# Block-sparse attention with a routed MLP on one core: where direct pairs are summed, and how selection flags are turned

## The chip, the cores and the metric

One core of a Trainium2 chip runs one launch of the kernel. The metric is the device time of that launch in microseconds (us), less is better. Before the change it is 269.96 us, the median of three runs (269.89 to 271.47).

## The reference, cut to what matters

Attention over 4 batches of 8 heads, 768 positions, head dimension 64. Keys are grouped into 24 chunks of 32. From the minimum and maximum of each chunk an upper bound of each query's scores is made; each query keeps its 6 best chunks. Its output, as 3072 rows of 512, goes through a mixture of 8 experts with at most 80 rows each. In outline:

```
ub = np.sum(np.maximum(q[..., None, :] * k_min[:, :, None], q[..., None, :] * k_max[:, :, None]), axis=-1)
ub = np.where(causal, ub, -1e9)
top_chunks = np.argsort(ub, axis=-1)[..., -6:]
scores = np.where(sel & causal_position, scale * q @ k.T, -1e9)
attn = np.exp(scores - max) ; attn = attn / (attn.sum(-1) + 1e-9)
x = (attn @ v) as rows of 512
e = argmax(x @ w_gate); keep the 80 rows of highest gate weight per expert
out[rows] = gate * (relu(x @ w1[e]) @ w2[e])     # other rows are 0
```

## The kernel before, in words

**Pairs.** Two heads make a pair, four pairs a batch, sixteen pairs (0 to 15) the attention. The loop `for i in range(NP)` (L1218) is written out at build time; the order of its calls is the order of each engine's queue. `Sync.op` (L72) records what each instruction reads and writes and puts in the waits; engines otherwise run their queues in order. All of pair i+1's preparation runs beside pair i.

**One pair.** A pair's scores are made transposed, keys on partitions and queries on columns, in six stages (`STEPS`, L179). For each stage `scores` (L575) issues TensorE matmuls of keys by queries (`score_mm`, L572, or L560 in half tiles), adds MASKV to the chunks that a query has not selected by a second matmul (`flags`, L594: the table of blocks `ind` by the turned flags `unsT`), and lets ScalarE write the exponential to EXB (L604). Score buffers SC0 and SC1 alternate, so stage 2 can write SC0 only when the exponential of stage 0 has read it. For early pairs a 512-column score matmul of stages 0 and 1 is issued as two of 256 (L566). GpSimd then masks the diagonal block (`select`, L656 and L653) and adds the stages up into ES, one 768-column sum per head (`fold`, L672; the pieces are listed in `ADDS`, L190); some adds are VectorE's (`own_fold`, L675). `values` (L707) multiplies the exponentials by v on TensorE (L717) in twelve groups, and ScalarE copies the two parts of the output to oT (`values_out`, L725). `sums` (L744) makes, in the next pair's turn, the rows' denominators from ES (L753) and the routing logits from oT (L730) in the accumulator M0; its last matmul frees ES, into whose first tile GpSimd's first mask of the next pair writes.

**Short and direct pairs.** Pairs 1 to 5, 8, 9 and 13 are short: their last two stages share buffers in a tighter order, and `rows` (L801), which turns the previous pair's output, comes between the first score matmuls and their flags. Pairs 5, 9 and 13 are direct: `fold` leaves two of their adds out, which `sums` makes up for by matmuls that read the exponentials themselves (L748). After a direct pair, stage 2 of the next pair is issued before `sums` (L1226, L1227), its mask and fold later (L1245).

**Flags.** For the next pair, TensorE computes the bounds (`bounds`, L483); in `bounds_out` VectorE transposes them, finds the six best by MAX8 (L497) and writes the flags of unselected chunks to `uns` (L502): for each of five query tiles and each head a block of 64 columns of which 24 count. `unselT` (L505) turns them: for pairs 1 to 15 ten TensorE transposes (five tiles by two heads, L521) into MB, and one ScalarE copy of 640 columns to `unsT` (L523). `unselT(i + 1)` is called after `values(i)` (L1322), so the copy queues on ScalarE behind the values' second output copy. The next user is `flags` of stage 0 of pair i+1. Pair 0 has a turn of its own (L512, L517), with two copies of 384 and 256 columns.

**Routing.** Between the stages stand pieces of the previous batch's routing: VectorE's compares (`rank_cmp`, L931, and `rank_diag`, L924) at the end of the second pair of a batch, the counting matmuls that read them (`rank_count`, L1062) in the third pair, `rank_late` (L1076 and after) on VectorE, and table matmuls (L1085) in the fourth. In the last batch's third pair (14) the table comes after the values.

**Start.** POOL writes the block table `ind` from 64 partitions at a time (L419, L421) while the first loads run; ScalarE's first work of pair 0 is L454. After pair 15, a tail gathers the selected rows and runs the eight experts (`up`, L1457; `down`, L1483).

## Time and profile before

| what | value |
|---|---|
| median of the runs (3) | 269.96 us |
| the profiled execution, own time | 270.17 us |
| its span in the trace | 268.2 us |
| TensorE's granted clock, all 40 slices | 9 tenths or more of full speed (2.4 GHz) |
| busy share: TensorE / VectorE / GpSimd / ScalarE | 95% / 80% / 77% / 58% |
| DMA engines' mean busy share | near 90% until the tail |

The profile is of one execution. Times in a timeline are us from the span's start; PE is TensorE's matmul side, PEld its weight loads (which run ahead of the matmuls), DVE VectorE, ACT ScalarE, POOL GpSimd, SP the load queue. A row of a timeline may merge several instructions of one line (xN): its first number is when the first starts, its second from there to the end of the last. A float32 matmul is two instructions. What stands in brackets is how long the engine was idle before and what released it; with several waits the one that came last.

### The profile page before, as it was taken

To read this page: it belongs to the slowest core of one execution; us is meant where nothing else is said; L and a number is where in the kernel's file an instruction comes from. 1 tells how busy PE (TensorE), PEld (TensorE's weight loads), DVE (VectorE), ACT (ScalarE), POOL (GpSimd) and SP (SyncE) were. 2 spreads that over 40 slices of the span, in tenths; PEclk is the share of its full clock that TensorE was granted. 3 is DMA by queue.
4 is the path that set the end of the run, shared out by engine and by line. 5 is a ranking of instruction groups with operands and counts; after the bars stand their busy time and mean duration, and the time that the engine had idled before them with its cause. 6 is when DMAs were issued, how large, how long until landed. Compare 5 with 4: busy or idle time off the path is not lost.

```text
span 268.2 us, 9821 instructions
## 1 busy us (share of the span) xinstructions
PE 256.0 (95%) x4152; PEld 167.2 (62%) x4152; DVE 214.8 (80%) x587; ACT 155.4 (58%) x243; POOL 207.6 (77%) x291
## 2 busy tenths in 40 slices
PE   7799999999999999999999999999999999988993
PEld 7367676767676565666665666666556557664663
DVE  6878787687989988859899889999998998953242
ACT  2286757575777654657776456564865576841220
POOL 6068959895999798969997999888998942725852
PEclk9999999999999999999999999999999999999999
DMA  9979999999999999997999889969999991911771
GB/s 148 173 128 165 142 293 195 298 222 222 151 200 205 226 160 197 206 221 147 164 186 222 150 147 210 212 112 295 287 243 218 215 190 9 197 44 47 152 150 65
DMA packets 148618, 48.38 MB, mean 180 GB/s; under 512 B 131583, under 2 KB 138870, under 8 KB 148512
## 3 DMA queue, kind: packets, MB, share of 16 engines
q1 hardware_dynamic: 113552, 23.23, 44.5%
q0 software_dynamic: 9936, 18.64, 36.9%
q10 hardware_dynamic: 25088, 5.90, 10.9%
q8 instruction: 32, 0.52, 0.8%
q14 instruction: 10, 0.08, 0.1%
HBM read 57.03 MB, written 11.01 MB: 254 GB/s over the span
## 4 chain that ended last, share of the span: by engine, by line
PE 73%; POOL 11%; DVE 5%; DMA 4%; ACT 3%; issue 2%; ACTq 1%; DVEq 0%
PE OB L717 22%; PE SC L572 13%; POOL ES L672 8%; PE SC L560 7%; PE SC L594 5%; PE OB L1483 4%; PE SC L1457 4%; PE MM L483 4%; PE MM L753 3%; ACT EXB L604 3%; DMA qn<-x_rows,idx 3%; PE MM L730 2%; POOL EXB L656 2%; PE OB L801 2%; DMA qn<-in_q_dram 1%
## 5 line engine op out<-in xcount | busy, mean ns | idle before, releaser
L604 ACT ACTIVATE EXB<-SC 128x1024 f32<-128x1024 f32 (+2 forms) x87 | 81.2, 947 | 35.9 <-PE SC L594 14.4
L672 POOL TENSOR_TENSOR ES<-ES,EXB 128x512 f32<-128x512 f32 (+1 forms) x76 | 80.4, 1060 | 5.1
L717 PE MATMUL OB<-EXB,vn 128*64 128x256 f32 (+2 forms) x640 | 69.6, 365 | 0.8 <-POOL EXB L656 0.7
L572 PE MATMUL SC<-qT,kT 64*128 64x256 f32 (+3 forms) x356 | 61.2, 450 | 0.1
L717 PEld LDWEIGHTS OB<-EXB,vn 128*64 128x64 f32 x640 | 42.9, 137 | 23.3 <-issue 7.5
L672 POOL TENSOR_TENSOR ES<-EXB 128x512 f32<-128x512 f32 (+1 forms) x29 | 45.0, 1551 | 1.8
L594 PE MATMUL SC<-unsT,ind 64*128 64x320 bf16 (+9 forms) x286 | 34.9, 303 | 0.4
L572 PEld LDWEIGHTS SC<-qT,kT 64*128 64x128 f32 x356 | 29.1, 187 | 8.9 <-issue 4.4
L725 ACT ACTIVATE oT<-OB 128x512 f32<-128x512 f32 (+1 forms) x32 | 15.7, 490 | 31.6 <-PE OB L717 31.6
L656 POOL TENSOR_SCALAR_AFFINE_SELECT EXB<-EXB 128x256 f32<-128x256 f32 x63 | 27.5, 442 | 5.5 <-ACT EXB L604 5.5
L656 POOL TENSOR_SCALAR_AFFINE_SELECT ES<-EXB 128x256 f32<-128x256 f32 x15 | 7.3, 484 | 22.3 <-PE MM L753 14.9
L594 PEld LDWEIGHTS SC<-unsT,ind 64*128 64x128 bf16 (+1 forms) x286 | 12.3, 100 | 17.9 <-issue 8.2
L560 PE MATMUL SC<-qT,kT 64*64 64x256 f32 (+5 forms) x256 | 21.7, 436 | 0.0
L450 DVE STREAM_TRANSPOSE qT<-qn 128x768 f32<-128x768 f32 x16 | 15.5, 971 | 5.8 <-PE SC L594 5.0
L454 ACT ACTIVATE rq<-qT 128x768 f32<-128x768 f32 x16 | 13.5, 845 | 9.7 <-DVE qT L450 9.2
L460 DVE STREAM_TRANSPOSE kT<-kn 128x768 f32<-128x768 f32 x16 | 15.5, 968 | 1.4 <-DMA kn<-in_k_dram 1.2
L462 DVE TENSOR_REDUCE kmm<-kT 128x24 f32<-128x768 f32 x16 | 15.3, 953 | 0.5
L465 DVE TENSOR_REDUCE kmx<-kT 128x24 f32<-128x768 f32 x16 | 15.1, 941 | 0.0
L497 DVE MAX8 top<-MM 128x8 f32<-128x8 f32 (+4 forms) x160 | 14.6, 164 | 0.6
L828 DVE TENSOR_TENSOR xp<-OB,rden 128x768 bf16<-128x768 f32 x14 | 13.3, 953 | 0.4
L739 DVE STREAM_TRANSPOSE MM<-MM 128x192 f32<-128x192 f32 x16 | 6.3, 394 | 8.3 <-PE MM L753 8.0
L753 PE MATMUL MM<-ES,onc 128*32 128x192 f32 x240 | 12.5, 326 | 0.0
(269 smaller groups left out, 457.4 us busy)
## 6 DMA issues: line engine op xcount, KB each, us to landing
w1s<-in_moe_w_dram POOLq DMA_DIRECT2D x8, 1024.0 KB, 10.0
w2s<-in_moe_w_dram POOLq DMA_DIRECT2D x7, 1024.0 KB, 14.3
kn<-in_k_dram SPq DMA_DIRECT2D x62, 96.0 KB, 3.7
qn<-in_q_dram SPq DMA_DIRECT2D x62, 96.0 KB, 3.9
vn<-in_v_dram ACTq DMA_DIRECT2D x28, 192.0 KB, 4.9
out_dram<-w1s SPq DMA_DIRECT2D x2, 1536.0 KB, 7.3
out_dram<-out_dram SPq DMA_DIRECT2D x2, 1536.0 KB, 9.8
x_rows<-xp SPq DMA_DIRECT2D x7, 384.0 KB, 4.3
```

Source lines behind the costliest of these rows:

```text
L450: op("dve", lambda: ve.transpose(qT[j][:], qn[s][:].rearrange("p a b c -> p (a b c)")), r=[f"qn{s}{g}" for g in range(4)], w=[f"qT{j}"])
L460: op("dve", lambda: ve.transpose(kT[j][:], kn[s][:].rearrange("p a b c -> p (a b c)")), r=[f"kn{s}{g}" for g in range(4)], w=[f"kT{j}"])
L462: op("dve", lambda: ve.tensor_reduce(kmm[j][:, 0, 0:NCH], kv, AX, ALU.min), r=[f"kT{j}"], w=[f"kmm{j}"])
L560: op("pe", lambda: pe.matmul(o, kT[j][pr, k0:k0 + 64], qT[j][pr, q0 + cut:q1], start=not flags, stop=bool(flags)), r=[f"kT{j}", f"qT{j}"], ...
L572: op("pe", lambda: pe.matmul(o, kT[j][pr, ts(kt)], qT[j][pr, x0:x1], start=not flags and (not cols or cols[0] == 0) and n == 0, stop=bool( ...
L594: op("pe", lambda: pe.matmul(ps[ot, h * 512 + c0 + x:h * 512 + c1], ind[pr, k0:k0 + (64 if halves else 128)], unsT[j][pr, b0 - 128 + x:q1 ...
L604: op("act", lambda: ac.activation(Ex(st, None, 0, W, turned(i)), src, ACTF.Exp, scale=SCALE), r=pk, w=[f"E{st}"])
L656: op("gp", lambda: gp.affine_select(ad, a, pattern=[[0, 2], [1, 128]], compare_op=ALU.is_ge, fill=0.0, base=0, channel_multiplier=-1), r=[ ...
L672: op(e, lambda: sy.queue[e].tensor_tensor(o, in0, in1, ALU.add), r=[f"E{s2}", f"E{first[0]}"] if first else [f"E{s2}"] + (["E5"] if (s2, c ...
L717: op("pe", lambda: pe.matmul(OB[pr, q0:q1], vs[:, kt - RT, h, :] if kt >= RT and turned(i) else vn[s][:, kt, h, :], ex, start=(n == 0), st ...
L725: op("act", lambda: ac.activation(oT[:, q0:q1], OB[:, q0:q1], ACTF.Copy), r=[f"O{bk}"], w=[f"oT{bk}"])
L753: op("pe", lambda: pe.matmul(M0[c * 32:c * 32 + 32, 0:192], onc[:, h, :], stripes(ES, h * S + c * 32, 0, 0, None), start=False, stop=(h == ...
```

## The change

In part it concerns how flags are turned. `uns` is laid out so that two query tiles of one head lie side by side (32 columns each), and one transpose turns both: three blocks by two heads, six transposes. Each block then holds an even tile's flags on one half of its 64 partitions and an odd tile's on the other. ScalarE copies it twice, with a per-partition scale `par` of ones and zeros: once keeping the even tiles (384 columns), once the odd ones (256). The block table `ind` is repeated in both halves, its second copies made by ScalarE at the start (five small memsets on VectorE make `par`). The flags' matmuls keep their shapes. In six turns (after pairs 5, 6, 9, 10, 11, 13) `unselT(i + 1)` is called from inside `values(i)`, ahead of its last two groups. Pair 0's turn stays. The other part concerns direct pairs: stage 2 of the next pair is no longer ahead of `sums`, and the add of (4, 384) to columns 640 to 768 leaves GpSimd's list; `sums` reads that piece by sixteen TensorE instructions of 32 columns. The cut of score matmuls in two reaches further (pairs 6 and 7, and stage 0 of pair 8).

```diff
@@ -251,7 +251,7 @@
                 top8 = al(pers, "top8", [128, NT - 1, 2, 8])
-                uns = al(pers, "uns", [128, NT - 1, 2, D], BF16)
+                uns = al(pers, "uns", [128, (NT - 1) * 2 * D], BF16)
                 unsT = [al(pers, "unsT", [128, (NT - 1) * 128], BF16) for _ in range(2)]
@@ -276,7 +276,8 @@
                 ind = al(pers, "ind", [128, NT * 128], BF16)
-                cb = al(pers, "cb", [128, 4])
+                cbp = al(pers, "cb", [128, 8])
+                cb, par = cbp[:, 0:4], cbp[:, 4:6]
                 wg = al(pers, "wg", [128, NPB, 32])
@@ -399,13 +400,16 @@
                 op("dve", lambda: ve.memset(wg[:], 0.0), w=["wg"])
+                op("dve", lambda: ve.memset(par, 0.0), w=["par"])
+                for g in range(4):
+                    op("dve", lambda: ve.memset(par[g * 32:g * 32 + 32, g % 2:g % 2 + 1], 1.0), r=["par"], w=[f"par{g}"])
                 op("dve", lambda: ve.memset(onc[:], 0.0), w=["onc"])
...
                 op("gp", lambda: gp.iota(vc, pattern=[[CHUNK, 4]], base=0, channel_multiplier=-1), w=["tc"])
-                op("dve", lambda: ve.tensor_scalar(cb[:], vc, 0, NEGSEL, ALU.is_gt, ALU.mult), r=["tc"], w=["cb"])
+                op("dve", lambda: ve.tensor_scalar(cb, vc, 0, NEGSEL, ALU.is_gt, ALU.mult), r=["tc"], w=["cb"])
@@ -415,11 +419,13 @@
                 for h in range(2):
-                    o = ind[h * 64:(h + 1) * 64, :]
+                    o = ind[h * 64:h * 64 + 32, :]
                     op("gp", lambda: gp.affine_select(o, o, pattern=[[1, S]], compare_op=ALU.is_ge, fill=0.0,
...
                                                       base=CHUNK - 1, channel_multiplier=CHUNK), r=[f"ind{h}"], w=[f"ind{h}"])
+                for h in range(2):
+                    op("act", lambda: ac.activation(ind[h * 64 + 32:h * 64 + 64, :], ind[0:32, :], ACTF.Copy), r=["ind", "ind0"], w=[f"ind{h + 2}"])
                 WG = ["wg0", "wg1"]
@@ -490,37 +496,43 @@
                     dg = bass.AP(MM, 196, [[1024, 128], [160, 2], [36, NT - 1], [1, 4]])
-                    cbv = bass.AP(cb, 0, [[4, 128], [0, 2], [0, NT - 1], [1, 4]])
+                    cbv = bass.AP(cbp, 0, [[8, 128], [0, 2], [0, NT - 1], [1, 4]])
                     op("dve", lambda: ve.tensor_tensor(dg, dg, cbv, ALU.add), r=["ubm0", "ubm1", "cb"], w=["ubm"])
...
                     thr = bass.AP(top8, 5, [[(NT - 1) * 16, 128], [8, 2], [16, NT - 1], [0, NCH]])
-                    un = bass.AP(uns, 0, [[(NT - 1) * 2 * D, 128], [D, 2], [2 * D, NT - 1], [1, NCH]])
+                    un = bass.AP(uns, 0, [[(NT - 1) * 2 * D, 128], [NT * 32 if i else D, 2], [32 if i else 2 * D, NT - 1], [1, NCH]])
                     uv = bass.AP(MM, 192, [[1024, 128], [160, 2], [32, NT - 1], [1, NCH]])
...
                     j = i % 2
+                    HB = NT // 2
+                    PK = ["par"] + [f"par{g}" for g in range(4)]
                     if i == 0:
...
                                 pr = slice(u * 64, u * 64 + 64)
-                                op("pe", lambda: pe.transpose(mh[u][:, t * 64:t * 64 + 64], uns[pr, t, :, :].rearrange("p a b -> p (a b)"), ident_bf[pr, pr]),
+                                op("pe", lambda: pe.transpose(mh[u][:, t * 64:t * 64 + 64], bass.AP(uns, u * 64 * (NT - 1) * 2 * D + t * 2 * D, [[(NT - 1) * 2 * D, 64], [1, 2 * D]]), ident_bf[pr, pr]),
                                    r=["uns", "ident_bf"], w=["M0", "MB"], inc=(t == NT - 2 and u == 1))
...
                         return
-                    for t in range(NT - 1):
+                    for b2 in range(HB):
                         for h in range(2):
-                            op("pe", lambda: pe.transpose(MB[h * 64:h * 64 + 64, ts(t)], uns[:, t, h, :], ident_bf[:]),
-                               r=["uns", "ident_bf"], w=["MB"], inc=(t == NT - 2 and h == 1))
-                    op("act", lambda: ac.activation(unsT[j][:], MB[:, 0:(NT - 1) * 128], ACTF.Copy), r=["MB"], w=[f"unsT{j}"])
+                            op("pe", lambda: pe.transpose(MB[h * 64:h * 64 + 64, ts(b2)], uns[:, h * NT * 32 + b2 * 64:h * NT * 32 + b2 * 64 + 64], ident_bf[:]),
+                               r=["uns", "ident_bf"], w=["MB"], inc=(b2 == HB - 1 and h == 1))
+                    for g, key in ((0, f"unsT{j}"), (1, f"unsU{j}")):
+                        n = HB - g
+                        dst = bass.AP(unsT[j], g * 128, [[(NT - 1) * 128, 128], [256, n], [1, 128]])
+                        op("act", lambda: ac.activation(dst, MB[:, 0:n * 128].rearrange("p (t c) -> p t c", c=128), ACTF.Copy, scale=par[:, g:g + 1]),
+                           r=["MB"] + PK, w=[key])
@@ -563,7 +575,7 @@
                         parts = [(q0, q1)]
-                        if st < 2 and mid(i) and (i - 1) * 2 + st < 10:
+                        if st < 2 and mid(i) and (i - 1) * 2 + st < 15:
                             parts = [(q0, q0 + 256), (q0 + 256, q1)]
@@ -593,7 +605,7 @@
                                                            start=first, stop=not first),
-                                   r=[f"ind{h}", f"unsT{j}"] + (["unsTb"] if i == 0 and st else []), w=pk, inc=inc)
+                                   r=[f"ind{h}", f"ind{h + 2}", f"unsT{j}", f"unsU{j}"] + (["unsTb"] if i == 0 and st else []), w=pk, inc=inc)
@@ -662,7 +674,7 @@
                 def fold(st, e="gp", i=0):
-                    for (s2, c2, q0, q1) in [a for a in ADDS[st] if i in (0, NP - 1) or a != (4, 0, 384, 512) and not ((direct(i) or i in WPLAN or i in (1, 3)) and a == (5, 0, 640, 768)) and (a != (4, 128, 512, 768) or i not in (1, 2, 3))]:
+                    for (s2, c2, q0, q1) in [a for a in ADDS[st] if i in (0, NP - 1) or a != (4, 0, 384, 512) and not ((direct(i) or i in WPLAN or i in (1, 3)) and a == (5, 0, 640, 768)) and (a != (4, 128, 512, 768) or i not in (1, 2, 3)) and not (direct(i) and a == (4, 384, 640, 768))]:
                         n = q1 - q0
@@ -704,11 +716,13 @@
-                def values(i, bks=(0, 1), ns=(0, 9), out=True):
+                def values(i, bks=(0, 1), ns=(0, 9), out=True, mid=None):
                     s = i % NB
...
                     for g, (bk, n) in enumerate(order):
+                        if mid and g == len(order) - 2:
+                            mid()
                         kt, q0, q1, st, c = lists[bk][n]
@@ -748,6 +762,11 @@
                                r=["onc0", "onc1", "E4", "E5"], w=["M0"], inc=False)
+                    for h in range(2):
+                        for c in range(4) if direct(i) else ():
+                            op("pe", lambda: pe.matmul(M0[c * 32:c * 32 + 32, 160:192], onc[:, h, :], bass.AP(
+                                EXB, 4992 + h * 256 + c * 32, [[EXP, 128], [1, 32]]), start=False, stop=False),
+                               r=["onc0", "onc1", "E5"], w=["M0"], inc=False)
                     for h in range(2):
@@ -1223,8 +1242,6 @@
                         clear_xg("k", 0)
-                    if direct(i - 1):
-                        scores(i, 2, 3, False)
                     if i:
@@ -1242,9 +1259,7 @@
                         rank_cmp(bb, 5, 4)
-                    if direct(i - 1):
-                        folds(i, 2)
-                    scores(i, 3 if direct(i - 1) or not i else 2, 4)
+                    scores(i, 2 if i else 3, 4)
                     if i == 0:
@@ -1313,12 +1328,13 @@
                             clear_xg(n, s)
-                    values(i)
+                    early = i in (5, 6, 9, 10, 11, 13)
+                    values(i, mid=(lambda: unselT(i + 1)) if early else None)
                     if i == NP - 2:
...
                         vw_turn()
-                    if i + 1 < NP:
+                    if i + 1 < NP and not early:
                         unselT(i + 1)
...
                         rank_row(bb)
```

## Rows read from the trace of the kernel before

**Rows 1.** The page, engines: busy us (share of the span) xinstructions.

```profile
PE 256.0 (95%) x4152; PEld 167.2 (62%) x4152; DVE 214.8 (80%) x587; ACT 155.4 (58%) x243; POOL 207.6 (77%) x291
```

**Rows 2.** The list of waits: engine, line, releaser: total us, times, longest us.

```profile
PEld OB L717 <- issue: 10.9, 54, 0.3
...
PEld SC L594 <- ACT unsT L523: 3.5, 6, 0.6
```

**Rows 3.** The timeline of TensorE, pair 2's start and pair 5 to pair 6.

```profile
35.97 1.13 PE L572 MATMUL SC<-qT,kT 64*128 64x256 f32 x8
...
87.40 0.45 PE L521 MATMUL MM<-ident_bf,uns 128*64 128x128 bf16 x10
87.78 1.13 PE L572 MATMUL SC<-qT,kT 64*128 64x512 f32 x4
88.74 0.30 PE L594 MATMUL SC<-unsT,ind 64*128 64x320 bf16 x2
...
89.74 0.84 PE L594 MATMUL SC<-unsT,ind 64*128 64x448 bf16 x4
...
91.36 0.53 PE L730 MATMUL MM<-oT,wg 128*32 128x192 f32 x8
91.71 0.41 PE L748 MATMUL MM<-EXB,onc 128*32 128x64 f32 x16
91.94 0.83 PE L753 MATMUL MM<-ES,onc 128*32 128x192 f32 x16
...
93.99 0.28 PE L1062 MATMUL MM<-w2s,ohb 128*32 128x32 bf16 x8
```

**Rows 4.** The timeline of TensorE's weight loads: pairs 2, 6, 7 and 14.

```profile
37.24 0.11 PEld L594 LDWEIGHTS SC<-unsT,ind 64*128 64x128 bf16 x2
...
90.18 0.10 PEld L594 LDWEIGHTS SC<-unsT,ind 64*128 64x128 bf16 x2 [0.77 <-ACT EXB L604]
...
99.55 1.50 PEld L717 LDWEIGHTS OB<-EXB,vn 128*64 128x64 f32 x22 [0.58 <-POOL EXB L656]
...
108.39 0.30 PEld L1085 LDWEIGHTS MM<-RC,OHS 128*80 128x80 bf16 x6 [0.50 <-DVE lgp L818]
...
210.88 2.58 PEld L717 LDWEIGHTS OB<-EXB,vn 128*64 128x64 f32 x32 [1.01 <-POOL EXB L656]
```

**Rows 5.** TensorE's groups by shape: busy us, mean ns of one, idle before.

```profile
L521 PE MATMUL MM<-ident_bf,uns 128*64 128x128 bf16 x150 | 6.8, 220 | 0.0
```

**Rows 6.** The timeline of ScalarE, the turn into pair 2.

```profile
36.12 0.70 ACT L523 ACTIVATE unsT<-MM 128x640 bf16<-128x640 bf16 x1
```

**Rows 7.** The timeline of all engines, the first 24 us.

```profile
4.43 0.82 POOL L421 TENSOR_SCALAR_AFFINE_SELECT ind<-ind 64x768 bf16<-64x768 bf16 x1
...
7.59 0.84 ACT L454 ACTIVATE rq<-qT 128x768 f32<-128x768 f32 x1 [2.89 <-DVE qT L450]
...
12.17 0.77 ACT L517 ACTIVATE unsT<-MM 128x384 bf16<-128x384 bf16 x2 [3.74 <-PE MM L512]
```

**Rows 8.** ScalarE's groups by shape, an instruction with a one-value-per-partition bias.

```profile
L962 ACT ACTIVATE vn<-G,gt 128x640 bf16<-128x640 f32 x1 | 0.8, 817 | 0.0
```

**Rows 9.** The timeline of VectorE, pairs 5 and 6.

```profile
80.75 1.19 DVE L931 TENSOR_SCALAR w2s<-G,gt 128x640 bf16<-128x640 f32 x1
...
85.14 0.41 DVE L502 TENSOR_TENSOR uns<-MM,top 128x240 bf16<-128x240 f32 x1
...
90.50 2.66 DVE L931 TENSOR_SCALAR w1s<-G,gt 128x640 bf16<-128x640 f32 x4
```

**Rows 10.** GpSimd, timeline of pairs 5 and 6, then its groups from 89.8 to 90.9.

```profile
86.36 4.69 POOL L672 TENSOR_TENSOR ES<-ES,EXB 128x512 f32<-128x512 f32 x4
91.02 0.49 POOL L467 TENSOR_TENSOR kmm<-kmx,kmm 128x24 f32<-128x24 f32 x1
92.88 0.56 POOL L656 TENSOR_SCALAR_AFFINE_SELECT ES<-EXB 128x256 f32<-128x256 f32 x1 [1.37 <-PE MM L753]
...
93.88 1.82 POOL L672 TENSOR_TENSOR ES<-EXB 128x768 f32<-128x768 f32 x1
...
L672 POOL TENSOR_TENSOR ES<-ES,EXB 128x256 f32<-128x256 f32 x1 | 1.2, 1186 | 0.1
```

## The prediction, made before the changed kernel ran

> **What bounds the kernel now.** I read the page's table of engines first: TensorE is busy for 256.0 of 268.2 us [rows 1]. So time can leave in two ways only: fewer or shorter TensorE instructions, or shorter stretches in which TensorE waits. The list of waits comes second, for what it waits for: six waits of its weight loads for the turned flags, 3.5 us together, the longest kind that this change touches [rows 2]; not all of such a wait is lost, since the array still streams the matmul before. Third come the timelines of TensorE and of its weight loads around the step from pair 5 (a direct pair) to pair 6; there the reader is to see the order scores, flags, sums, and the price of each piece [rows 3, 4]. ScalarE, GpSimd and VectorE I read in the same stretch, for when flags, folds and compares are ready. Durations are of the profiled execution, 270.17 us, that is its span of 268.2 and 1.97 around it; the median of the runs shown is 269.96, 0.21 lower, and the forecast is put on that scale. A measurement of this kernel tells about 1% (2.7 us) from no change.
>
> **Part 1: flags turned two tiles at a time.** Each of the fifteen turns of pairs 1 to 15 loses 4 of its 10 TensorE transposes. In the turn into pair 6 the ten stand from 87.40 until the next scores at 87.78, 0.38 us [rows 3]. If all of it scaled, 4 x 0.038 = 0.15 us would go. But one instruction lasts 0.22 [rows 5], the ten together 0.45, so they follow each other at (0.45 - 0.22) / 9 = 0.026 us, and 4 x 0.026 = 0.10 goes, while the change-over to the scores stays. Fewer instructions can't cost, so the bounds are 0.10 and 0.15; I take 0.10, the pace of the rows.
>
> Against it, ScalarE now makes two masked copies instead of one, each with a scale from a table of one value per partition. One copy of 640 columns takes 0.70 [rows 6]. The first pair has the same split without the scale: 384 and 256 columns in 0.77 together [rows 7]. A ScalarE instruction of 640 columns that reads such a table (as its bias) takes 0.817 [rows 8], about 0.12 over the copy. So two copies take from 0.77 to 0.77 + 2 x 0.12 = 1.01; I take 1.01, as that row is the nearest with a table. In a turn such as that into pair 2 the copy starts at 36.12, so the flags are ready at 37.13; TensorE loads them at 37.24 [rows 4], 0.10 earlier in the new kernel. It just fits. So eight of the nine turns that stay after the values save 0.10; the last, into pair 15, whose copy waits for the transposes themselves, half: 0.85 together.
>
> The six turns that move ahead of the last two value groups (after pairs 5, 6, 9, 10, 11 and 13) go before five of the waits of rows 2 and one turn without such a wait. The scores of 4 x 512 columns need 0.85 at 2.4 GHz, but the flags come 0.96 after them (88.74 - 87.78) [rows 3]: 0.11 is lost today, since the copy of flags queues behind the copy of the values' output. Moved, the copies run beside the last value matmuls, ahead of that output copy. What they need is ready: VectorE's flags are written at 85.14 + 0.41 = 85.55 [rows 9], the transposes would come near 86.7. If that cover of 1.1 us were gone, value matmuls would queue behind the wait. The output copy starts some 0.5 later, and only the sums, 3 us on, read it. So 0.20 each for five and 0.10 for the sixth (sorting matmuls stand between): 1.10. Part 1 gives 1.95 us, between 1.5 and 2.75.
>
> The score matmuls cut in two (pairs 6, 7, and 8's first stage) cost nothing: eight of 256 columns take 1.13, four of 512 take 1.13 [rows 3]. The five added memsets and two copies of the block table at the start lie beside waiting: the table's first half is ready at 5.25 (4.43 + 0.82), ScalarE has been idle for 2.89 before its work at 7.59 [rows 7], and two copies of 768 columns at 0.84 end near 7.2, with the memsets added. Beyond that, each microsecond would be one of the path.
>
> **Part 2: direct pairs (5, 9, 13).** Their sums go back ahead of stage 2 of the next pair. Four terms.
>
> First, stage 2's flags wait today until ScalarE has emptied the score buffer (loaded at 90.18, wait 0.77) [rows 4]; the flags before them start at 89.74 and stream 448 columns in 0.19, so TensorE stands idle for 0.25. With the sums in between, that goes: 3 x 0.25 = 0.75.
>
> Second, the last fold as 16 matmuls (a float32 one is two instructions) of 32 columns per pair. The 16 of 64 columns take 91.94 - 91.71 = 0.23 [rows 3]. Half the columns lies between 0.11 and 0.23; I take 0.22, since 14 ns each looks like the pace of issue: -0.66.
>
> Third, GpSimd. The sums would start near 89.84 and read the folded tile at 89.84 + 0.58 + 0.22 = 90.64. GpSimd ends at 91.06, but its last fold is the one that goes, 1.19 long [rows 10]: the rest is done near 89.8, 0.8 us in time. Its first mask of pair 6 then starts some 91.36 - 89.84 - 0.22 = 1.3 us earlier than 92.88, where it has been idle for 1.37 [rows 10]. What that is worth stands in the values of pairs 6, 10 and 14, which wait for its late masks: 0.58 in the first, 1.01 in the last [rows 4], 0.61 between. The normal gap there is 10.9 / 54 = 0.20 [rows 2], so 0.38, 0.41 and 0.81 are lost. The first two go; in pair 14 VectorE's chain ends beside TensorE, so I take half of 0.81: 1.19 together.
>
> Fourth, the table matmuls of pairs 7 and 11 wait 0.50 for VectorE [rows 4], whose chain starts when GpSimd's folds of pair 6 end. With these earlier I take 0.2 each, as a part of such a gap is change-over: 0.4, between 0 and 1.0.
>
> Part 2: 0.75 - 0.66 + 1.19 + 0.4 = 1.68, between 0.1 and 3.0.
>
> **A rule weighed.** An earlier GpSimd meets VectorE's compares of pair 5's gates: four in 2.66 us, to 93.16 [rows 9], beside an idle GpSimd now. Beside a fold one such compare took 1.19 instead of 0.665 [rows 9]. The Trainium skill (Advanced Engine Details and Errata, GPSIMD Details) lets the two engines conflict only when VectorE's instruction has two inputs in SBUF or a mode that uses two ports. The compare has one tensor input, and at 0.665 us for 640 columns shows no doubled rate; by the rule it would lose nothing. The row disagrees, so the measurement decides. By the rule the compares end at 93.16, by the row 0.53 later; TensorE needs them at 93.99 less 0.10, 0.10, 0.25 and plus 0.22, that is 93.76, so the sum is the same by both.
>
> **Sum.** 1.95 + 1.68 = 3.6 us: 270.17 - 3.6 = 266.57, on the scale of the median 266.4.
>
> **Rivals.**
> - A, only the turns count: GpSimd's earlier start is given back, because VectorE or the values are late next anyway, and the direct pairs come out even. 269.96 - 1.95 = 268.0. For it: VectorE's chain in pair 14. Against: in pairs 6 and 10 the masks are what the values wait for. 0.20.
> - B, the two copies are late: they need more than 1.01 and the eight late turns give nothing, or their flags wait. 269.96 - (3.6 - 0.8) = 267.2. For it: the margin in pair 2 is nil. 0.08.
> - C, the sums wait for GpSimd after all: the spared fold isn't spared, because VectorE's two-input compares just before hold up the others. Then the folds end at 91.06 against 90.64: 3 x 0.42, and the masks start less early: 267.8. 0.06.
> - D, slower: GpSimd and VectorE exclude each other in pairs 6, 10 and 14. The last compare waits until the fold of 1.82 [rows 10] is through, near 93.88 + 1.82 - 1.34 = 94.36, and ends at 95.0; the counting matmuls at 93.76 wait 1.25, three times 3.75, and GpSimd, held up in turn, keeps the values' waits. Then 269.96 - 1.95 - 0.09 + 3.75 = 271.7. It decides from 1.2 us per pair on. For it: 1.19 beside a fold. Against: that is 0.53 more, not a whole fold, and 0.60 is free. 0.06.
>
> **How the numbers follow.** The forecast has 0.60, with its own range from 265.2 to 267.6; A 0.20, B 0.08, C 0.06, D 0.06. The best ends of all terms, 2.75 + 3.0, would give 264.2. The range of 264.7 to 269.2 leaves out that edge and D. Faster by over 1% means under 267.26: nine tenths of the forecast, half of B, a little of C and A: 0.64. Slower by over 1% is D, 0.06. The rest, 0.30, is within 1%.
>
> **What would show it.** Right: six L521-like transposes per turn and about 0.10 less from values to scores; no wait for flags in pairs 6, 7, 10, 11 and 14; sums at 89.8 of pair 6's clock without a wait for GpSimd; masks over a microsecond earlier; no 0.6 or 1.0 in the values of pairs 6, 10 and 14. Wrong: flags of pairs 2 to 4 that now wait for ScalarE, counting matmuls of pairs 6, 10 and 14 that wait for VectorE, or steps from pair to pair that shrink in the trace and a tail that grows by the same.

## The result and the profile after

The changed kernel takes 266.95 us (median; 266.76 to 267.36) against 269.96, a ratio of 0.988 with a 95% interval of 0.986 to 0.990. The forecast was 266.4. The profiled execution takes 267.16 us with a span of 265.2, 3.0 under the span of 268.2 before. So the size is nearly right. The way to it is not: by the steps counted below, most of the 3 us came from the part that was priced at 1.68, and little from the part priced at 1.95.

The page's engines, to be held against [rows 1] (TensorE lost 2.2 us of work, ScalarE gained 5.5):

```profile
PE 253.8 (96%) x4160; PEld 167.2 (63%) x4160; DVE 211.3 (80%) x592; ACT 160.9 (61%) x260; POOL 206.5 (78%) x288
```

The page's chain that ended last, by engine, of the kernel before:

```profile
PE 73%; POOL 11%; DVE 5%; DMA 4%; ACT 3%; issue 2%; ACTq 1%; DVEq 0%
```

and of the changed one; GpSimd has left the chain:

```profile
PE 87%; DMA 4%; ACT 4%; DVE 2%; issue 1%; ACTq 1%; POOL 0%; DVEq 0%
```

The lists of waits say the same. Before, with the values' waits for GpSimd's masks in the list:

```profile
PEld OB L717 <- POOL EXB L656: 3.7, 9, 1.0
```

After; masks are now L668, values L731, flags L606 (the counterpart of the second line of [rows 2]), ScalarE's copies of flags L534:

```profile
PEld SC L606 <- ACT unsT L534: 1.5, 4, 0.8
...
PEld OB L731 <- POOL EXB L668: 0.6, 2, 0.3
```

TensorE's timeline after, pair 5 to pair 6, against [rows 3]:

```profile
87.67 1.13 PE L584 MATMUL SC<-qT,kT 64*128 64x256 f32 x8
88.64 0.30 PE L606 MATMUL SC<-unsT,ind 64*128 64x320 bf16 x2
...
89.92 0.53 PE L744 MATMUL MM<-oT,wg 128*32 128x192 f32 x8
90.27 0.41 PE L762 MATMUL MM<-EXB,onc 128*32 128x64 f32 x16
90.50 0.31 PE L767 MATMUL MM<-EXB,onc 128*32 128x32 f32 x16
90.62 0.84 PE L772 MATMUL MM<-ES,onc 128*32 128x192 f32 x16
...
93.65 0.28 PE L1081 MATMUL MM<-w2s,ohb 128*32 128x32 bf16 x8
```

The flags still come 0.97 after the scores (88.64 - 87.67; 0.96 before), though nothing waits for them now. The sums start at 89.92 (forecast 89.84). The 16 new instructions (L767, eight float32 matmuls) take 0.12, from 90.50 to 90.62, not 0.22. Counting matmuls start at 93.65 (forecast 93.76).

GpSimd and VectorE in the same stretch, against [rows 10] and [rows 9]:

```profile
86.35 3.44 POOL L684 TENSOR_TENSOR ES<-ES,EXB 128x512 f32<-128x512 f32 x3
...
91.62 0.41 POOL L668 TENSOR_SCALAR_AFFINE_SELECT ES<-EXB 128x256 f32<-128x256 f32 x1 [1.05 <-PE MM L772]
91.98 0.66 POOL L668 TENSOR_SCALAR_AFFINE_SELECT EXB<-EXB 128x256 f32<-128x256 f32 x1
92.72 1.95 POOL L684 TENSOR_TENSOR ES<-EXB 128x768 f32<-128x768 f32 x1
94.62 0.41 POOL L668 TENSOR_SCALAR_AFFINE_SELECT EXB<-EXB 128x256 f32<-128x256 f32 x1
```
```profile
90.51 2.48 DVE L950 TENSOR_SCALAR w1s<-G,gt 128x640 bf16<-128x640 f32 x4
```

Folds end at 89.79, the first mask starts 1.26 earlier than before (91.62 against 92.88).

To see where the time went I cut the span at the first matmul of each pair's values (TensorE's timeline, first line of L731, L717 before) and added up the steps by kind. "Predicted" puts the prediction's terms into the same bins; a turn into pair k falls into the step from k-1 to k. The last two columns are kernels explained below.

```
steps (values to values)      before   after  change  predicted  sums alone  turns alone
up to the first values         18.09   18.30   +0.21     0          -0.02       +0.15
0 to 4                         51.54   51.06   -0.48    -0.40       -0.09       -0.48
4-5, 8-9, 12-13 (gate rows)    39.77   40.26   +0.49    -0.30       -0.11       +0.51
5-6, 9-10, 13-14               43.37   42.34   -1.03    -0.69       -0.59       -0.32
6-7, 10-11                     28.22   26.92   -1.30    -1.59       -1.09       -0.07
7-8, 11-12                     27.17   26.96   -0.21    -0.20        0.00       -0.21
14-15                          18.22   17.51   -0.71    -0.45       +0.15       +0.08
from pair 15's values on       41.82   41.85   +0.03     0          -0.15       -0.16
```

Three bins stand out: the turns into pairs 5 and 9 cost time (0.27 and 0.24; the step into 13 gains 0.02), the start looks longer, and in the last step neither half shows the gain of the whole (the kernel with the sums alone has a stall there, told below).

### The profile page after: what moved, and what is told of

It reads as the page before. It is cut to its first block, busy times and chain, and to the rows that moved or that the text cites. A ratio compares the mean times of both kernels' runs of the same rounds, so it can differ in the third digit from the quotient of the medians.

```text
span 265.2 us, 9859 instructions
## 1 busy us (share of the span) xinstructions
PE 253.8 (96%) x4160; PEld 167.2 (63%) x4160; DVE 211.3 (80%) x592; ACT 160.9 (61%) x260; POOL 206.5 (78%) x288
## 4 chain that ended last, share of the span: by engine, by line
PE 87%; DMA 4%; ACT 4%; DVE 2%; issue 1%; ACTq 1%; POOL 0%; DVEq 0%
PE OB L731 27%; PE SC L584 19%; PE SC L572 7%; PE SC L606 6%; PE MM L489 4%; PE OB L1499 4%; PE SC L1473 4%; PE MM L772 4%; PE MM L744 3%; DMA qn<-x_rows,idx 3%; PE OB L820 2%; DMA qn<-in_q_dram 2%; ACT EXB L616 1%; PE OB L572 1%; PE MM L811 1%; PE MM L529 1%
## 5 line engine op out<-in xcount | busy, mean ns | idle before, releaser
L684 POOL TENSOR_TENSOR ES<-ES,EXB 128x512 f32<-128x512 f32 (+1 forms) x73 | 77.6, 1066 | 4.9
L731 PE MATMUL OB<-EXB,vn 128*64 128x256 f32 (+2 forms) x640 | 69.3, 364 | 0.0
L731 PEld LDWEIGHTS OB<-EXB,vn 128*64 128x64 f32 x640 | 42.2, 137 | 21.0 <-issue 8.3
L584 PEld LDWEIGHTS SC<-qT,kT 64*128 64x128 f32 x376 | 31.1, 187 | 12.1 <-issue 7.7
L606 PE MATMUL SC<-unsT,ind 64*128 64x320 bf16 (+9 forms) x286 | 34.9, 303 | 0.1
L668 POOL TENSOR_SCALAR_AFFINE_SELECT EXB<-EXB 128x256 f32<-128x256 f32 x63 | 28.9, 465 | 5.0 <-ACT EXB L616 5.0
L668 POOL TENSOR_SCALAR_AFFINE_SELECT ES<-EXB 128x256 f32<-128x256 f32 x15 | 6.3, 419 | 20.5 <-PE MM L772 13.7
L606 PEld LDWEIGHTS SC<-unsT,ind 64*128 64x128 bf16 (+1 forms) x286 | 12.3, 100 | 14.1 <-issue 7.4
L534 ACT ACTIVATE unsT<-MM,cb 128x384 bf16<-128x384 bf16 (+1 forms) x30 | 14.2, 525 | 4.2 <-PE MM L529 4.0
```

Of the source, the lines that this page charges most:

```text
L584: op("pe", lambda: pe.matmul(o, kT[j][pr, ts(kt)], qT[j][pr, x0:x1], start=not flags and (not cols or cols[0] == 0) and n == 0, stop=bool( ...
L606: op("pe", lambda: pe.matmul(ps[ot, h * 512 + c0 + x:h * 512 + c1], ind[pr, k0:k0 + (64 if halves else 128)], unsT[j][pr, b0 - 128 + x:q1 ...
L668: op("gp", lambda: gp.affine_select(ad, a, pattern=[[0, 2], [1, 128]], compare_op=ALU.is_ge, fill=0.0, base=0, channel_multiplier=-1), r=[ ...
L684: op(e, lambda: sy.queue[e].tensor_tensor(o, in0, in1, ALU.add), r=[f"E{s2}", f"E{first[0]}"] if first else [f"E{s2}"] + (["E5"] if (s2, c ...
L731: op("pe", lambda: pe.matmul(OB[pr, q0:q1], vs[:, kt - RT, h, :] if kt >= RT and turned(i) else vn[s][:, kt, h, :], ex, start=(n == 0), st ...
```

## The experiments

Ratios are to the kernel before on the same chip, in five rounds each.

**Either part alone.** The kernel before with the sums in their old place and the 16 matmuls:

```diff
-                    if direct(i - 1):
-                        scores(i, 2, 3, False)
...
-                    if direct(i - 1):
-                        folds(i, 2)
-                    scores(i, 3 if direct(i - 1) or not i else 2, 4)
+                    scores(i, 2 if i else 3, 4)
```

> The kernel before with the second part of the change alone: the direct pairs' sums stand ahead of stage 2 of the next pair and their last fold is 16 TensorE matmuls; flags are turned as before. Theory now (the two traces: the steps around pairs 6, 10 and 14 give most of the 3.0): about 2.4 us are gained, 267.6. The prediction's own terms say 1.68, 268.3. A rival, that the sums only pay together with the early turns, says under 0.8, 269.2 or more.

Measured: 269.16, ratio 0.997 (0.994 to 1.000); the profiled execution took 268.27, the lowest of twelve. In the step from pair 14 to 15 this execution has a gap of 0.41 in the last sums that no releaser explains, and with what goes with it that piece is 0.63 longer than in the other kernels. Without it the bins up to pair 15's values add up to -2.4. So the steps of this one execution say what the theory says, while the median, 0.8 under the kernel before, lies where the rival put it. What the longer executions lose no trace shows, so whole times leave this rival open.

The changed kernel with these lines the other way round and the fold back on GpSimd:

> The changed kernel without its second part: sums of direct pairs behind stage 2 of the next pair, last fold by GpSimd; turns of two tiles, six of them early, the cut scores and the new start stay. Theory now (late turns give 0.05 to 0.15 each, the turns into pairs 5, 9 and 13 give back 0.25 to 0.35 each, the start 0.2): about 0.6 us gained, 269.4. The prediction's own terms say 1.95, 268.0.

Measured: 270.43, ratio 1.001 (1.000 to 1.003): nothing gained. The profiled execution, 269.64, is again one of the fastest. By steps -0.34 up to pair 15's values, of which +0.15 is the start. Early turns gain 0.10 to 0.11 in the steps into 6, 10, 14 and 12, not 0.20, and 0.01 and 0.06 in those into 7 and 11. TensorE's weight loads of this kernel show the old waits in place, for stage 2's exponential and for a mask of pair 14:

```profile
90.01 0.10 PEld L606 LDWEIGHTS SC<-unsT,ind 64*128 64x128 bf16 x2 [0.56 <-ACT EXB L616]
...
210.54 2.58 PEld L731 LDWEIGHTS OB<-EXB,vn 128*64 128x64 f32 x32 [1.10 <-POOL EXB L668]
```

The last of them is why the turns alone gain nothing in the step to pair 15: there GpSimd's masks, not TensorE, say when values go on (1.01 in [rows 4], 0.32 in the changed kernel). By medians the halves gain 0.8 and lose 0.5, and together they gain 3.0; by steps up to pair 15's values they gain 1.75 (2.4 without the stall) and 0.34, and together 3.03. The steps carry the account from here on, and they are those of one execution each.

**Turns not early.**

```diff
-                    early = i in (5, 6, 9, 10, 11, 13)
+                    early = False
```

> The changed kernel with all fifteen turns behind the values. Theory now (the 0.96 from scores to flags was no wait, so an early turn saves no more than a late one): within 0.3 of the changed kernel, 267.0 to 267.25. The prediction's own terms (0.10 more for an early turn in five, 0.05 in one) say 0.55 lost, 267.5; if the two copies, once late, come later than TensorE needs them, more, 268 or above.

Measured: 269.19, ratio 0.996 (0.995 to 0.998), 2.2 us over the changed kernel. The theory fell, and the prediction's own terms were too small; the third case is what happened, copies later than TensorE needs them. By steps it loses 0.42 or 0.43 into pairs 6, 10 and 14, 0.29 and 0.30 into 7 and 11, 0.15 into 12: 2.0 together. ScalarE and TensorE in the turn into pair 6:

```profile
87.58 0.38 ACT L739 ACTIVATE oT<-OB 128x256 f32<-128x256 f32 x1 [0.48 <-PE OB L731]
...
87.99 0.95 ACT L534 ACTIVATE unsT<-MM,cb 128x384 bf16<-128x384 bf16 x2
```
```profile
87.61 1.13 PE L584 MATMUL SC<-qT,kT 64*128 64x256 f32 x8
88.99 0.31 PE L606 MATMUL SC<-unsT,ind 64*128 64x320 bf16 x2 [0.25 <-ACT unsT L534]
```

The two copies wait for the output copy and end at 88.94; flags come 1.38 after the scores instead of 0.97. The one copy of 0.70 just reached the 0.97. So the early turn pays for the second copy; beyond that it is worth the 0.10 of the transposes. The list of waits of this kernel has 5.4 us in seven waits of that kind, against 1.5 in four.

**Gate rows first.** For pairs 4, 8 and 12:

```diff
-                    values(i, mid=(lambda: unselT(i + 1)) if early else None)
+                    values(i, mid=(lambda: unselT(i + 1)) if early else (lambda: rank_row(bb)) if live and kk == 0 else None)
...
-                    if live and kk == 0:
-                        rank_row(bb)
```

In the changed kernel the scores of pair 5's stage 1 wait at 76.31 for ScalarE's copy of the gate rows (L927), which is queued behind the two flag copies. ScalarE and TensorE's weight loads, changed kernel:

```profile
74.61 0.58 ACT L534 ACTIVATE unsT<-MM,cb 128x384 bf16<-128x384 bf16 x1
...
75.08 0.47 ACT L534 ACTIVATE unsT<-MM,cb 128x256 bf16<-128x256 bf16 x1
75.44 0.82 ACT L927 ACTIVATE G<-SC 128x768 f32<-128x768 f32 x1
```
```profile
76.31 0.73 PEld L584 LDWEIGHTS SC<-qT,kT 64*128 64x128 f32 x8 [0.36 <-ACT G L927]
```

> The changed kernel with the gate rows of pairs 4, 8 and 12 turned ahead of the last two value groups, so that ScalarE's copy of them stands ahead of the two flag copies. Theory: the waits of 0.36, 0.33 and 0.15 of the next pair's scores for that copy go, 0.8 us, 266.1. Rival: the turns into pairs 5, 9 and 13 are held by something beside it (VectorE's chain, the flag copies, which now come later), and the time stays at 266.95 or rises.

Measured: 267.37, ratio 0.992 (0.989 to 0.994), and 40.20 in the bin against 40.26: nothing gained, the rival is right. That wait is gone, but ScalarE's chain got no shorter. Its timeline in this kernel:

```profile
73.96 0.81 ACT L927 ACTIVATE G<-SC 128x768 f32<-128x768 f32 x1 [0.30 <-PE SC L924]
74.79 0.38 ACT L739 ACTIVATE oT<-OB 128x256 f32<-128x256 f32 x1
...
75.20 0.94 ACT L534 ACTIVATE unsT<-MM,cb 128x384 bf16<-128x384 bf16 x2
```

Now the flag copies end at 76.14 and the flags, not the next scores, come last, at 76.19.

**The turns into 5 and 9 early too**, which puts the flag copies ahead instead:

```diff
-                    early = i in (5, 6, 9, 10, 11, 13)
+                    early = i in (4, 5, 6, 8, 9, 10, 11, 13)
```

> The changed kernel with the turns into pairs 5 and 9 also ahead of the last two value groups. Theory: ScalarE's chain behind the values (output copy 0.38, two flag copies 0.95 instead of 0.70, gate rows 0.82) is what costs 0.25 in each of these two steps (13.45 and 13.41 from values to values against 13.18 and 13.17 before); with the flag copies ahead both come to 13.1 and the time to 266.4. Rival: VectorE's flags (ready at 72.99, the turn would start at 73.1) or something else holds the step, and it stays at 13.4.

Measured: both steps at 13.07, as expected; so ScalarE's chain is the cause. ScalarE and TensorE:

```profile
73.81 0.95 ACT L534 ACTIVATE unsT<-MM,cb 128x384 bf16<-128x384 bf16 x2
74.64 0.38 ACT L739 ACTIVATE oT<-OB 128x256 f32<-128x256 f32 x1
...
74.91 0.82 ACT L927 ACTIVATE G<-SC 128x768 f32<-128x768 f32 x1
```
```profile
75.98 0.76 PEld L584 LDWEIGHTS SC<-qT,kT 64*128 64x128 f32 x8
```

The gate rows are copied by 75.73, and the scores at 75.98 wait for nothing. The time was 265.16, but on a chip where the kernel before takes 267.95 too: ratio 0.988 (0.983 to 0.993). I ran it again:

> The changed kernel with the turns into pairs 5 and 9 early as well, nothing else, once more, because stalls without a releaser spread its first times by 3 us. Steps into pairs 5 and 9 at 13.07; ratio to before 0.985 (0.988 less 0.7 of 270). If it comes out at 0.988 or above, the two steps' gain is given back in whole times.

Measured: 267.36 against 270.25, ratio 0.988 (0.987 to 0.990). Both steps are at 13.07 again, but the step from pair 9 to 10 took 14.89 instead of the 14.11 of the same program's first profile: TensorE's weight loads stop in the middle of pair 9's bounds and nothing in the profile releases them.

```profile
150.23 0.15 PEld L489 LDWEIGHTS MM<-rq,kmm 64*32 64x32 f32 x7 [0.66 <-issue]
```

So two steps are shorter by 0.35 each in both profiles, and whole times don't show it. A version that beats the changed kernel by a measurable amount was not found.

**The fold back on GpSimd**, sums in the old place (the exception in `fold` goes too):

```diff
-                        for c in range(4) if direct(i) else ():
-                            op("pe", lambda: pe.matmul(M0[c * 32:c * 32 + 32, 160:192], onc[:, h, :], bass.AP(
-                                EXB, 4992 + h * 256 + c * 32, [[EXP, 128], [1, 32]]), start=False, stop=False),
```

> The changed kernel with the last fold of the direct pairs on GpSimd again, without the 16 added matmuls; the sums stay in their old place. Theory: GpSimd ends its folds 1.15 later, near 90.95 instead of 89.79 in pair 6, the sums want them at 90.5, so TensorE waits some 0.45 and saves 0.12, and the masks start 0.35 later, which the values of pairs 6, 10 and 14 feel: about 0.5 per direct pair, 268.5. Rival (GpSimd has room): no wait, 0.12 gained three times, 266.6.

Measured: 268.39 against 267.95, ratio 1.001 (0.998 to 1.003). TensorE's weight loads and GpSimd at pair 6:

```profile
91.07 0.48 PEld L767 LDWEIGHTS MM<-ES,onc 128*32 128x32 f32 x16 [0.57 <-POOL ES L684]
```
```profile
86.32 4.69 POOL L684 TENSOR_TENSOR ES<-ES,EXB 128x512 f32<-128x512 f32 x4
...
92.09 0.71 POOL L668 TENSOR_SCALAR_AFFINE_SELECT ES<-EXB 128x256 f32<-128x256 f32 x1 [0.63 <-PE MM L767]
```

The sums wait, as the theory said. By steps it is 0.49 or 0.50 in each of three, 0.13 or 0.14 in each of two and 0.18 in the last: 1.9 us. The ratio says 3.3 (1.25% of 268); on this chip the stretch after pair 15's values took anything from 39.2 to 41.4 us in four kernels that don't differ there, so 1.9 is the better number.

**Late sums, fold on TensorE**, the fourth corner: the changed kernel with the first experiment's lines back.

```diff
+                    if direct(i - 1):
+                        scores(i, 2, 3, False)
...
-                    scores(i, 2 if i else 3, 4)
+                    if direct(i - 1):
+                        folds(i, 2)
+                    scores(i, 3 if direct(i - 1) or not i else 2, 4)
```

> The changed kernel with the direct pairs' sums behind stage 2 of the next pair again, their last fold still 16 TensorE matmuls. Theory: neither half of the second part pays alone; GpSimd, rid of the fold, waits for the later sums, TensorE gets 0.12 more to do: values to values 14.45 in the step from pair 5 to 6 and 14.05 in the next (14.35 and 14.08 with the turns alone, 14.12 and 13.47 with both halves), time as the kernel with the turns alone, ratio to before 1.001 to 1.003. Rival: a shorter GpSimd queue is worth most by itself: 13.6 in the step from pair 6 to 7, ratio 0.993 or lower.

Measured: 269.51, ratio 0.998 (0.997 to 1.000), between theory and rival. The two steps that the expectation names came out at 15.01 and 13.47, but in the first of them eight score instructions at 95.75 take half a microsecond longer than in the kernel with the turns alone, with no releaser, and GpSimd catches up meanwhile; so they say nothing. The steps from pair 9 to 11, free of stalls in all four corners, add up to 28.42 (late sums, fold on GpSimd), 28.32 (late, TensorE), 28.20 (old place, GpSimd) and 27.56 (old place, TensorE). The old place alone is worth 0.22, the fold alone 0.10, both 0.86. GpSimd, done early, just waits for the late sums:

```profile
92.71 0.41 POOL L668 TENSOR_SCALAR_AFFINE_SELECT ES<-EXB 128x256 f32<-128x256 f32 x1 [2.34 <-PE MM L772]
```

**The start.** The five memsets moved:

```diff
                 bounds_out(0)
+                op("dve", lambda: ve.memset(par, 0.0), w=["par"])
+                for g in range(4):
+                    op("dve", lambda: ve.memset(par[g * 32:g * 32 + 32, g % 2:g % 2 + 1], 1.0), r=["par"], w=[f"par{g}"])
```

> The changed kernel with the five memsets of the mask table moved on VectorE from the start to behind the first pair's bounds, so that its memset of the block table starts 0.6 earlier, as before. Theory A: the 0.2 by which the first values come later (18.24 to 18.30 in four kernels with the new start, 18.07 and 18.09 in two with the old one) comes from VectorE's longer start: first values at 18.08, time 0.2 lower, 266.75. Theory B: it is in the first loads or in ScalarE's two copies: first values stay at 18.25 or later.

Measured: 265.88 against 267.95, ratio 0.988 (0.984 to 0.993), first values at 18.26: not VectorE's memsets. Its time says little, as the stretch after pair 15's values took 39.4 us here, while two steps of its profile are longer: 14.15 from pair 4 to 5 (13.45 in the changed kernel), explained below, and 13.78 from pair 0 to 1 (12.72). In the latter a load of gate weights lands late, VectorE's copy of them falls behind a fold of GpSimd's, and TensorE's next turn waits 1.11 for the flags. The copy ends 0.04 after the fold (18.90 against 18.86):

```profile
17.63 1.27 DVE L1210 COPY wg<-wgr 64x32 f32<-64x32 f32 x1
```
```profile
17.58 1.28 POOL L681 TENSOR_TENSOR ES<-EXB 128x512 f32<-128x512 f32 x1
```

Then the changed kernel again, and one with the turns into 5 and 9 early and the table built as before:

```diff
-                    o = ind[h * 64:h * 64 + 32, :]
+                    o = ind[h * 64:(h + 1) * 64, :]
...
-                    op("act", lambda: ac.activation(ind[h * 64 + 32:h * 64 + 64, :], ind[0:32, :], ACTF.Copy), r=["ind", "ind0"], w=[f"ind{h + 2}"])
```

> The changed kernel itself, on the chip of this call, for comparison: ratio to before 0.988; steps from values to values within 0.05 of those known, but for a stall without a releaser here or there.

> The changed kernel with the turns into pairs 5 and 9 early, and with the block table built by GpSimd on all 128 partitions as before, without ScalarE's two copies. Steps into pairs 5 and 9 come out at 13.07 again and the time 0.7 under the changed kernel of the same call (ratio 0.9855). For the start: if ScalarE's two copies cause the later first values, these return to 18.08; if the first loads land later for another reason, they stay at 18.2 to 18.4.

In the latter the table's rows for the second tile of a block stay zero, so every second tile's unselected chunks go unmasked; but for the two copies the work is the same in kind and size. Measured: 267.02, ratio 0.988 (0.985 to 0.990), first values at 18.11; and 266.00, ratio 0.989 (0.984 to 0.994), first values at 18.02, both early steps at 13.07 or 13.06. The latter's median is 1.0 under that of the changed kernel on the same chip, where 0.7 was expected, but two of its six executions (268.46 and 269.52) lift its ratio. So the same changed kernel had its first values at 18.30 once and at 18.11 once. What differs is when the first keys land. VectorE, changed kernel, first and second profile:

```profile
4.90 0.98 DVE L466 STREAM_TRANSPOSE kT<-kn 128x768 f32<-128x768 f32 x1 [0.84 <-DMA kn<-in_k_dram]
```
```profile
4.72 0.98 DVE L466 STREAM_TRANSPOSE kT<-kn 128x768 f32<-128x768 f32 x1 [0.66 <-DMA kn<-in_k_dram]
```

In all fourteen profiles the first values come 13.39 or 13.40 after these keys, so nothing in between got longer. The keys themselves are there at 4.72 to 5.01 where ScalarE copies the table (eleven profiles) and at 4.63 to 4.70 in the three kernels that build it the old way. As the changed kernel alone spans 4.72 to 4.90, most of the 0.2 is not the change's; whether a few hundredths are, no run shows.

**Both at once**: the turns into 5 and 9 early, late memsets, and in pair 12 the gate rows first.

```diff
+                    values(i, mid=(lambda: unselT(i + 1)) if early else (lambda: rank_row(bb)) if i == 12 else None)
...
-                    if live and kk == 0:
+                    if live and kk == 0 and i != 12:
                         rank_row(bb)
```

> The changed kernel with both edits that should help: the turns into pairs 5 and 9 early, the five memsets behind the first bounds; and in pair 12 the gate rows turned ahead of the last two value groups. Theory: 0.25 + 0.25 + 0.2 + 0.05 add up, 266.2. Rival: a step that is made shorter is given back in pair 14, where GpSimd's masks already hold the values by 0.32: 266.6 or more.

Measured: 265.13 against 267.95, ratio 0.987 (0.983 to 0.992): not told apart from the changed kernel, and the rival's place (pair 14) was wrong too: that step stayed at 17.50. In its profile two other steps are longer: 0.8 from pair 9 to 10 with a gap like that at 150.23 above (0.69 here), and 0.7 from pair 4 to 5, which the kernel with late memsets alone has as well. VectorE and GpSimd at pair 4's gates, this kernel:

```profile
68.25 0.47 DVE L873 TENSOR_TENSOR lg<-lg,lmax 128x48 f32<-128x48 f32 x1
68.76 1.33 DVE L879 SCALAR_TENSOR_TENSOR oh<-lg,rank_c 128x48 f32<-128x48 f32 x1
```
```profile
68.24 0.42 POOL L665 TENSOR_SCALAR_AFFINE_SELECT EXB<-EXB 128x256 f32<-128x256 f32 x1
68.75 1.27 POOL L681 TENSOR_TENSOR ES<-ES,EXB 128x512 f32<-128x512 f32 x1
```

and the kernel with the early turns alone (the same lines are L876 and L882 there):

```profile
68.15 0.21 DVE L876 TENSOR_TENSOR lg<-lg,lmax 128x48 f32<-128x48 f32 x1
...
68.39 0.29 DVE L882 SCALAR_TENSOR_TENSOR oh<-lg,rank_c 128x48 f32<-128x48 f32 x1
```
```profile
68.17 0.46 POOL L668 TENSOR_SCALAR_AFFINE_SELECT EXB<-EXB 128x256 f32<-128x256 f32 x1
68.71 1.29 POOL L684 TENSOR_TENSOR ES<-ES,EXB 128x512 f32<-128x512 f32 x1
```

An instruction of VectorE with two SBUF inputs that starts 0.01 after GpSimd's ends just behind GpSimd's (68.72 against 68.66 for the mask, 70.09 against 70.02 for the fold); one that starts 0.02 ahead takes its 0.21. The 0.29 is such a wait too, of an instruction that takes 0.21 at its shortest: it starts while the mask runs and ends 0.05 after it (68.68 against 68.63), just ahead of the fold. Here 0.03 us of relative timing decide over 1.04 us of VectorE, and the flags behind it come 0.7 late. That the moved memsets are what shifts it is likely, as both kernels with them have it and no other has, but by which path no run shows.

## Why the prediction was nearly right, step by step

**Turns, 1.95 predicted: 0.3 to 0.9 measured by steps** (-0.34 alone; -1.28 on top of the sums, less 0.63 of the stall, give 0.65, or 0.9 with the start left out).

- Late turns save 0.10 each: right in sum for pairs 1 to 4 (0.48 for four, though 0.19, 0.06, 0.05 and 0.18 one by one) and for pair 8 (0.11).
- "It just fits": this is the step that failed. For the flags themselves it nearly held: into pair 2 the copies end at 37.21, and the flags come 1.39 after the scores (37.27 - 35.88) instead of 1.33; pairs 3 and 4 lose the same 0.05 or 0.06, pairs 1 and 8 nothing. ScalarE, changed kernel:

```profile
36.26 0.95 ACT L534 ACTIVATE unsT<-MM,cb 128x384 bf16<-128x384 bf16 x2
```

  But it looked only at the copies' own reader. In the turns into pairs 5, 9 and 13 ScalarE has one more copy queued behind (gate rows, 0.82), and TensorE's next scores write where that copy reads. The second flag copy (0.95 for both; 1.01 was forecast, 0.70 before) pushes it 0.25 late (into 13 the scores wait only 0.15 for it). The bin came out at +0.49 instead of -0.30: 0.79, more than the whole miss of 0.6.
- "0.11 is lost today": wrong. Five waits of [rows 2] sit behind a matmul that the array still streams; with the wait gone flags came 0.97 after the scores, with it 0.96. The early turns save 0.10 each or less, and their use is to cover the second copy, worth 2.0 us against late ones.
- The turn into pair 15: flags wait 0.81 for the copies, so it saves nothing; 0.05 was forecast.
- The cut score matmuls cost nothing: uncut, in pairs 10 and 11 of the changed kernel, whose turns are early as well, flags follow 0.96 after the scores (142.38 - 141.42 and 156.49 - 155.53).
- The start: hidden, as forecast, but the cover is used up. ScalarE, changed kernel:

```profile
5.87 1.71 ACT L428 ACTIVATE ind<-ind 32x768 bf16<-32x768 bf16 x2 [1.29 <-POOL ind L425]
7.78 0.84 ACT L460 ACTIVATE rq<-qT 128x768 f32<-128x768 f32 x1 [0.21 <-DVE qT L456]
```

The copies end at 7.58, not 7.2, because GpSimd's first half waits for a longer VectorE; 0.21 of idle time is left of 2.89, and none in the second profile, where the keys land earlier.

**Sums, 1.68 predicted: 2.2 alone, 2.7 on top of the turns, by steps.** The first is the sum of the steps from 5 to 7, from 9 to 11 and from 13 on, with the stall taken out (0.76 + 0.69 + 0.71); the second is the changed kernel against the turns alone in the same steps (0.84 + 0.86 + 1.03). The stage-2 wait less the new matmuls was to give 3 x 0.25 - 3 x 0.22 = 0.09; the bin with the sums alone has 0.59. The new matmuls cost 0.12 and not 0.22, which is 0.30 of it: instructions of half the columns took half the time, the lower bound and not the pace of issue. Masks and table: 1.19 for pairs 6 and 10, 1.09 measured; here the reasoning held, and so did the 0.8 us that GpSimd was to be in time, as the 0.57 shows that TensorE waits without it. In pair 14 half of the wait was credited (0.40); 0.48 came with the sums alone and 0.71 with both, since there GpSimd was behind by more than either half makes up.

**The rule weighed.** "The row disagrees" was too quick, and so was the reading of 2.66 as four times 0.665. Taken one by one (narrow stretches of VectorE's timeline, kernel before), a compare beside an idle GpSimd takes 0.55, and the first of the four takes 0.90:

```profile
90.50 0.90 DVE L931 TENSOR_SCALAR w1s<-G,gt 128x640 bf16<-128x640 f32 x1
...
92.61 0.55 DVE L931 TENSOR_SCALAR w1s<-G,gt 128x640 bf16<-128x640 f32 x1
```

That first one ends at 91.40, 0.35 after the folds of [rows 10] (91.05). The compare of 1.19 in [rows 9] ends at 81.94, 0.34 after this fold:

```profile
79.77 1.83 POOL L672 TENSOR_TENSOR ES<-EXB 128x768 f32<-128x768 f32 x1
```

All six compares of the kernel before that start during a fold end 0.34 to 0.36 after it. So a compare with one tensor input is held by the whole fold, and 1.19 was the rest of a fold. In the changed kernel the two take turns. The third compare meets the mask of 91.62 and ends 0.35 after it (92.38 against 92.03); GpSimd's next mask takes 0.66, where the same form takes 0.41 at 94.62, and the fold 1.95 against 1.82 in [rows 10].

```profile
91.69 0.69 DVE L950 TENSOR_SCALAR w1s<-G,gt 128x640 bf16<-128x640 f32 x1
```

VectorE lost nothing (2.48 against 2.66), and the last compare ended at 92.99, before the counting matmuls' 93.65. The sum was the same by rule and row, as said, but by order and not by room: the last compare starts at 92.41, 0.31 ahead of the fold. The Trainium skill (Advanced Engine Details and Errata, GPSIMD Details) has the two conflict for two SBUF inputs or a two-port mode. The rows of pair 4's gates above agree for the two inputs. The prediction excluded the mode by the 0.665; as 640 columns in 0.55 are well under the pace of VectorE's 768 columns in 0.94 to 0.98, the compare may run in a faster mode, and then rule and row agree. Which mode it runs in no run here shows.

**The rivals.** A (only the turns count) had it the wrong way round. B (late copies) is what happens in the turns into 5, 9, 13 and 15, by 0.05 or 0.06 in those into 2 to 4, and in the six early ones if none is early. C is what the fold's removal prevents. D's mechanism is real, for the compares too; what kept its price away is that the last compare came before the long fold, where D had it behind. That was a matter of 0.31 us, which the prediction didn't work out.

The bins' errors add up: 0.79 (gate rows), 0.21 (start) and 0.29 (steps 6-7 and 10-11) too hopeful; 0.34 (5-6 and the like), 0.26 (14-15) and 0.09 too careful; -3.63 + 1.29 - 0.69 = -3.03. A total that is right to 0.6 was built on terms that were off by more; that it came so close is in part luck.

## What to carry to other kernels

When an instruction on a busy in-order engine gets longer, follow every instruction queued behind it to its reader, not only its own: the price was paid by a copy that the change doesn't touch. A wait of a weight load is lost time only if the matmul before it has stopped streaming; compare the spacing of the matmuls with and without it before crediting it. Two edits that each free a different engine can be worth nearly three times their sum (0.86 against 0.22 and 0.10) when either engine alone still holds the step, so time all corners before dropping one.

## What the hardware showed that was not expected

- VectorE and GpSimd wait for each other as a whole, and the one that starts first goes first: 0.21 to 0.29 became 1.33 for an instruction of 48 columns that started 0.01 after a fold, a compare of 0.55 became 0.90 or 1.19, always ending 0.34 to 0.36 after the fold, and GpSimd's mask of 0.41 became 0.66 behind a compare.
- Stalls without a releaser: 0.41 in the last sums of one kernel, 0.66 in pair 9's bounds of another, in one execution and not in the other of the same program. They move whole times by as much as a 0.7 us edit. The Trainium skill (Runtime: NRT & Kernel Launch, Instruction fetch mechanics) says that each engine fetches its instructions in blocks by a DMA queue of its own, mostly hidden; whether these gaps are such fetches no run here shows.
- The same stretch after pair 15's values took 39.2 to 41.4 us on one chip and 41.7 to 42.2 on the others, in kernels that don't differ there; the kernel before took 267.95 on that chip against 269.8 to 270.3.
- Sixteen matmul instructions of 32 columns follow each other at 0.12 / 16 = 7.5 ns, the sixteen of 64 at (90.50 - 90.27) / 16 = 14 ns: at these sizes TensorE's pace still went with the columns.
